# Scaling dO and making half of the first group's A products on GpSimd instead of VectorE

## The chip, the cores and the metric

The kernel runs on one core of one Trainium2 chip. The metric is the device time in microseconds of one launch. Its engines are TensorE (PE in the profile, with its weight loads listed apart as PEld), VectorE (DVE), ScalarE (ACT), GpSimd (POOL) and SyncE (SP), which here only issues DMAs.

## The reference

The forward function mixes two branches by a gate; the kernel computes the output and the gradients with respect to all weights and x, given `grad_out` (dO). S = 2048 tokens, D = 576, F = 4608, all inputs in bf16.

```python
def _A_ref(x, w_r, w_i):
    X = rfft2(x.astype(float32), axes=(-2, -1))
    X = X * (w_r + 1j * w_i)
    return irfft2(X, s=(S, D), axes=(-2, -1)).astype(bfloat16)

def _B_ref(x, w_gate, w_up, w_down):
    return (gelu(x @ w_gate) * (x @ w_up)) @ w_down

g = sigmoid((x * gate_w).sum(-1, keepdims=True))
out = g * _A_ref(x, w_r, w_i) + (1 - g) * _B_ref(x, w_gate, w_up, w_down)

out, vjp = jax.vjp(f, x, w_r, w_i, w_gate, w_up, w_down, gate_w)
return out, *vjp(grad_out)
```

In branch B, with `A = gelu(x w_gate) * (x w_up)`, the gradient of `w_down` is `A^T ((1 - g) dO)`. This is where the scaled dO and the A product, the two things that the change moves, meet.

## The kernel before

**The layout.** The 2048 tokens are 16 row tiles of 128 (T = 16). `xn` holds x and `dB` holds dO in this layout, each 128 x 16 x 576 in SBUF. Both are transposed at the start by TensorE into `xT` and `dOT`; the transposes of `dB` are done by 50 us.

**The head** (to about 55 us) builds the tables for the Fourier transforms (`build_D`, `build_R`, `build_B`: most of it on VectorE, a part of `build_D` on GpSimd), transposes x and dO, computes the first half of the forward transform of x, and the gate g with `omg32` = 1 - g in f32, one column per row tile.

**The first phase** loops over 18 groups g of 256 hidden columns (`NG`, `FG`), and within a group over four steps m (`NPR`), each of which handles four row tiles as two pairs, tp = 2m and 2m + 1. A step does this:
- `H_mm` puts the matmuls of z = dO w_down^T and of the two products x w_gate and x w_up (`xy`) on TensorE's queue.
- `H_da` scales z by `omg32` on ScalarE (line 345).
- `H_q` and `H_ew1` square and copy `xy` on ScalarE and start the polynomial of the gelu on VectorE (lines 351 to 361).
- `H_ew2` (lines 372 to 393) runs two sigmoids on ScalarE and then eight VectorE instructions for each pair: lines 380 to 387, in this order. Line 382 makes `xb` = gelu(x w_gate), line 383 makes `A` = `xb` * `hu`, and lines 384 to 387 make the two other results, `dHg` and `dHu`. A later `flush` stores all three to HBM from SyncE's queue.
- Units of the Fourier branch (`fft_next`) are put between these. In the first group they are those of `fwd_units`: two matmul sets `u1` (line 492) and `u2` (lines 506 to 509) per row tile. A `u1` result is copied out of PSUM by ScalarE (line 498). A `u2` result is copied out by VectorE for the first eight row tiles (line 512, `Vt`) and by ScalarE for the others. In the first group there are four such units per step and more in the first.

The order on each engine is the order in which this program writes the instructions; there is no scheduler. In the first group there is no other work. From the second group on, each step also runs units of the weight gradients of the group before (`W_units`): `u_dw` and `tail` (lines 442 and 455), and `u_dwd` (line 425), which multiplies A by the scaled `dB`. Their results leave through GpSimd's DMA queue (lines 435, 448, 461, 462), which is the only thing that GpSimd does in that stage. The first `u_dwd` runs in step m = 1 of the second group, at 121.55 us in the trace.

**The scaling of dO.** `u_dwd` needs `dB` multiplied by `omg32`, in place. `scale_dB(n)` (line 793) does this for the next n row tiles, one instruction of 128 x 576 each (line 795). The kernel calls it twice, for eight tiles each: at the end of step m = 3 of the first group and at the end of step m = 0 of the second:

```python
if (g, m) in ((0, 3), (1, 0)):
    scale_dB(T // 2)
```

**The second phase** starts after 1010 us: it reads A, dHg and dHu back from HBM, transposed, and computes the outputs with long chains of matmuls (line 950).

Of the kernel before, what the change touches and what calls it, by code (L numbers as in the profile page):

```python
# [10 lines left out]
ALU = mybir.AluOpType  # L11
# [9 lines left out]
P, T = 128, 16  # L21
# [151 lines left out]
def kernel(  # L173
# [4 lines left out]
    nc = tc.nc  # L178
    LD = nc.sync
    ST = nc.gpsimd  # L180
    V = nc.vector
# [26 lines left out]
    dB = wstack.enter_context(tc.tile_pool(name="pdB", bufs=1)).tile([P, T, D], BF16, name="dB")  # L208
# [58 lines left out]
    omg32 = res.tile([P, T], F32, name="omg32")  # L267
# [42 lines left out]
    def H_mm(g, m):  # L310

        wgu, wdT = wts[g]
        ts = range(4 * m, 4 * m + 4)
        z = pz.tile([P, 2, 2, FG], F32, tag="z", name="z")

        def zo(t):
            return z[:, t % 2, t % 4 // 2, :]
        for t in ts:
            for ci in range(4):
                nc.tensor.matmul(zo(t), lhsT=dOT[:, ci, t, :], rhs=wdT[:, ci, :], start=(t % 4 < 2 and ci == 0), stop=False)  # L320
        for t in ts:
            r = (LO, HI)[t % 2]
            nc.tensor.matmul(zo(t), lhsT=dOT[r, 4, t, :], rhs=wdT[r, 4, :], start=False, stop=t % 4 >= 2)  # L323
        xy = [ph.tile([P, 2, 2 * FG], F32, tag="xy", name="xy") for _ in range(2)]
        for t in ts:
            r = (LO, HI)[t % 2]
            nc.tensor.matmul(xy[t % 4 // 2][:, t % 2, :], lhsT=xT[r, 4, t, :], rhs=wgu[r, 4, :], start=True, stop=False)  # L327

        def full(k):
            for t in ts[2 * k:2 * k + 2]:  # L330
                for ci in range(4):
                    nc.tensor.matmul(xy[k][:, t % 2, :], lhsT=xT[:, ci, t, :], rhs=wgu[:, ci, :], start=False, stop=(ci == 3))  # L332
            return xy[k]
        return z, full

    def ewt(tag):
        return ew.tile([P, TPB, FG], BF16, tag=tag, name=tag, bufs=3 if tag in ("da", "xb") else 2)

    def H_da(m, z):
        das = []  # L340
        for k in range(2):
            da = ewt("da")
            for tt in range(TPB):
                t = 4 * m + 2 * k + tt
                nc.scalar.activation(da[:, tt, :], z[:, tt, k, :], ACT.Copy, scale=omg32[:, t:t + 1])  # L345
            das.append(da)
        return das

    def H_q(xy):
        q = ewt("q")  # L350
        nc.scalar.activation(q[:], xy[:, :, 0:FG], ACT.Square)  # L351
        return q

    def H_ew1(xy, q):
        xb, s, hu = (ewt(n) for n in ("xb", "s", "hu"))
        nc.scalar.copy(xb[:], xy[:, :, 0:FG])  # L356
        nc.scalar.copy(hu[:], xy[:, :, FG:2 * FG])
        V.tensor_scalar(s[:], q[:], A_GELU, 1.0, op0=ALU.mult, op1=ALU.add)  # L358
        V.tensor_tensor(s[:], xb[:], s[:], op=ALU.mult)  # L359
        V.tensor_scalar(q[:], q[:], 6.0 * A_GELU * C_GELU, 2.0 * C_GELU, op0=ALU.mult, op1=ALU.add)  # L360
        V.tensor_tensor(q[:], xb[:], q[:], op=ALU.mult)
        return xb, q, s, hu
# [3 lines left out]
    def flush(n=9):  # L366

        while stores and n:
            stores.pop(0)()
            n -= 1  # L370

    def H_ew2(g, tp, tiles, da):
        xb, q, s, hu = tiles
        om = ewt("om")
        nc.scalar.activation(om[:], s[:], ACT.Sigmoid, scale=-2.0 * C_GELU)  # L375
        nc.scalar.activation(s[:], s[:], ACT.Sigmoid, scale=2.0 * C_GELU)  # L376
        A = keepA.tile([P, TPB, FG], BF16, tag="A", name="A")
        dHg = keep.tile([P, TPB, FG], BF16, tag="dHg", name="dHg")
        dHu = keep.tile([P, TPB, FG], BF16, tag="dHu", name="dHu")
        V.tensor_tensor(om[:], om[:], q[:], op=ALU.mult)  # L380
        V.tensor_scalar(om[:], om[:], 1.0, None, op0=ALU.add)
        V.tensor_tensor(xb[:], xb[:], s[:], op=ALU.mult)
        V.tensor_tensor(A[:], xb[:], hu[:], op=ALU.mult)
        V.tensor_tensor(om[:], om[:], s[:], op=ALU.mult)
        V.tensor_tensor(om[:], om[:], hu[:], op=ALU.mult)
        V.tensor_tensor(dHg[:], da[:], om[:], op=ALU.mult)
        V.tensor_tensor(dHu[:], da[:], xb[:], op=ALU.mult)
        fsl = slice(g * FG, (g + 1) * FG)
        def store():
            for k, tl in enumerate((A, dHg, dHu)):  # L390
                LD.dma_start(scr[k][tp][:, :, fsl].rearrange("t p f -> p t f"), tl[:])
        stores.append(store)
        kept.setdefault(g, []).append((A, dHg, dHu))
# [366 lines left out]
    def fft_next():  # L760
        while fft_pos[0] < len(fft):
            u = fft[fft_pos[0]]
            fft_pos[0] += 1
            u()
            if not getattr(u, "noslot", False):
                return
# [6 lines left out]
    def want(pr):  # L773

        n0 = 4 * NPR
        n = 4 * (pr + 1) if pr < NPR else n0 + (n_slots - n0) * (pr + 1 - NPR) / (LASTP - NPR)
        return int(min(n, n_slots) + 1e-9)
# [14 lines left out]

    def scale_dB(n):
        for t in range(scaled[0], min(scaled[0] + n, T)):
            V.tensor_scalar(dB[:, t, :], dB[:, t, :], omg32[:, t:t + 1], None, op0=ALU.mult)
            scaled[0] = t + 1

    for g in range(NG):
        if g == 1:
            pgs.close()  # L800
            pw = ps1.enter_context(tc.tile_pool(name="pw", bufs=2, space=PSUM, **kw))
        for m in range(NPR):
            pr = g * NPR + m
            n = want(pr) - done[0]
            done[0] += n
            hs = [h for u in pend[m] for h in u] if pend else []

            def side_work():
                for _ in range(3):
                    if side:  # L810
                        side.pop(0)()
            if g == 0 and m > 0:
                fft_next()
            z, xy_full = H_mm(g, m)
            xy = xy_full(0)
            das = H_da(m, z)
            q = H_q(xy)
            flush()
            if n:
                fft_next()  # L820
                n -= 1
            if pr == 0:
                fft_next()
            ta = H_ew1(xy, q)
            state = []

            def sig0():
                H_ew2(g, 2 * m, ta, das[0])
                side_work()
                state.append(None)  # L830

            def second():
                xy = xy_full(1)
                if g == 0:
                    fft_next()
                state.insert(0, H_ew1(xy, H_q(xy)))

            def sig1():
                H_ew2(g, 2 * m + 1, state[0], das[1])
                side_work()  # L840
            if g == 0:
                second()
                fft_next()
                sig0()
                sig1()
            else:
                jobs = [(0, sig0)] * bool(carry) + carry + [(1.7, second)] + [(0, sig0)] * (not carry) + hs
                us = sum(j[0] for j in jobs)
                at, k, late = 0.0, 1, [sig1]
                for w, f in jobs:  # L850
                    if k <= n and at > 0 and at >= k * us / (n + 1) - 0.6:
                        fft_next()
                        k += 1
                        if len(state) == 2 and late:
                            late.pop()()
                    f()
                    at += w
                while k <= n:
                    fft_next()
                    k += 1  # L860
                if late:
                    sig1()
            carry = []
            flush(len(stores) - 1)
            if m < 3 and g + 1 < NG:
                load_w(g + 1, m)
            if pr == 3:
                LD.dma_start(gwb[:], gate_w.partition_broadcast(P))
            if (g, m) in ((0, 3), (1, 0)):
                scale_dB(T // 2)  # L870
            if done[0] == n_slots or (pr >= wgT_from and pr % 2 == 0 and len(wgT_all) < 20):
                load_wgT()
                if done[0] == n_slots:
                    load_wgT()
        carry = pend[4] if pend else []
        pend = W_units(g)
# [223 lines left out]
```

## Time and profile before

The median of three runs is 1461.26 us (1460.99 to 1462.75). The profiled execution spans 1460.1 us.

| engine | busy us | share of the span |
|---|---|---|
| PE (matmuls) | 1429.2 | 98% |
| PEld (weight loads) | 1065.0 | 73% |
| DVE | 846.9 | 58% |
| ACT | 686.8 | 47% |
| POOL | 119.1 | 8% |

By stretches of about one step of the first group, and one after it (busy us of each engine):

| stretch, us | PE | DVE | ACT | POOL |
|---|---|---|---|---|
| 64 to 75 | 10.21 | 10.00 | 9.30 | 0.00 |
| 75 to 85 | 9.60 | 9.48 | 8.30 | 0.00 |
| 85 to 95 | 9.10 | 9.45 | 8.29 | 0.00 |
| 95 to 105 | 8.77 | 9.64 | 7.18 | 0.00 |
| 105 to 115 | 9.84 | 9.49 | 6.16 | 1.84 |

The instructions that the change touches are the 16 of line 795, 360 to 366 ns each, the first eight at 101.8 us and the last at 115.5, and the 144 of line 383 (8 a group, 424 to 427 ns), the first at 66.0 us.

How to read the views: the chain of work that ended last is followed back from the last instruction of the program, at each step to what released it, or to the instruction before it on its engine; its list in order of time gives start, length, engine, the tile written and the line. A timeline gives start, length, engine, line, operation, the tiles written and read, shapes and the count of instructions merged into the row, and in brackets the idle time of the engine ahead of it and what ended that. Successive instructions of one engine may overlap a little in the records. Two things that the program did at once stand in two timelines, one for each engine.

### The profile page before, as it was taken

How to read it: one execution, taken by the hardware profiler on the slowest of the kernel's cores; microseconds unless marked ns; L12 is line 12 of the kernel's file. 1: busy time of each engine (PE TensorE's matmuls, PEld its weight loads, DVE VectorE, ACT ScalarE, POOL GpSimd, SP SyncE). 2: the span in 40 equal slices, each digit the busy share in tenths (PEclk: the TensorE clock that was granted, in tenths of full speed). 3: DMA queues.
4: the chain of work that ended last, by engine and by line, in shares of the span. 5: the costliest groups of instructions: out<-in, count | busy, mean ns of one | idle time of the engine just before them, and what ended most of it. 6: DMA issues, size and time to landing. Idle time of an engine off the chain costs nothing.

```text
span 1460.1 us, 29983 instructions
## 1 busy us (share of the span) xinstructions
PE 1429.2 (98%) x11691; PEld 1065.0 (73%) x11776; DVE 846.9 (58%) x2258; ACT 686.8 (47%) x1355; POOL 119.1 (8%) x203
## 2 busy tenths in 40 slices
PE   7999999999999999999999999999999999999998
PEld 5766777667777677677677677768877777777776
DVE  7697677888887986777777776773000531212100
ACT  5776666766676666766766766662000000000000
POOL 1000011011011101001001000100000100000000
PEclk9999999999999999999999999999999999999999
DMA  5244344555445445434543544657999997788773
GB/s 191 63 125 123 114 126 120 140 146 139 137 138 150 119 116 138 129 107 111 142 128 102 139 127 122 173 135 165 262 193 199 219 199 162 170 157 165 153 151 72
DMA packets 501161, 210.54 MB, mean 144 GB/s; under 512 B 320951, under 2 KB 491129, under 8 KB 501017
## 3 DMA queue, kind: packets, MB, share of 16 engines
q1 hardware_dynamic: 491416, 188.10, 54.3%
q0 software_dynamic: 7792, 19.49, 4.4%
q8 instruction: 92, 1.51, 0.5%
q10 hardware_dynamic: 1808, 1.02, 0.3%
q14 instruction: 53, 0.43, 0.1%
HBM read 40.89 MB, written 93.82 MB: 92 GB/s over the span
## 4 chain that ended last, share of the span: by engine, by line
PE 91%; DVE 4%; issue 1%; ACT 1%; DMA 0%; DVEq 0%; ACTq 0%
PE acc L950 29%; PE wps L442 17%; PE xy L332 16%; PE wps L425 9%; PE z L320 8%; PE wps L455 2%; PE xy L327 2%; PE z L323 1%; PE pf L707 1%; PE pf L681 1%; PE pf L492 1%; PE pf L709 1%; PE fx L492 0%; DVE Vt L512 0%; DMA pin<-scr 0%
## 5 line engine op out<-in xcount | busy, mean ns | idle before, releaser
L950 PEld LDWEIGHTS <-pin 128*128 128x128 bf16 x3456 | 337.9, 98 | 87.0 <-DMA pin<-scr 2.0
L332 PE MATMUL xy<-wgu,xT 128*128 128x512 bf16 x1067 | 258.5, 379 | 9.4 <-issue 7.3
L442 PEld LDWEIGHTS <-xn 128*128 128x128 bf16 x2304 | 225.3, 98 | 32.4 <-issue 0.2
L332 PEld LDWEIGHTS <-xT 128*128 128x128 bf16 x1152 | 106.8, 98 | 137.3 <-issue 30.3
L345 ACT ACTIVATE da<-z,omg 128x256 bf16<-128x256 f32 x288 | 113.4, 475 | 147.4 <-PE z L323 144.3
L967 ACT COPY bo<-acc 128x288 f32<-128x288 f32 x32 | 12.8, 400 | 309.8 <-PE acc L950 309.8
L425 PE MATMUL wps<-dB,A 128*128 128x288 bf16 x1152 | 154.2, 286 | 0.0
L950 PE MATMUL acc<-wd_all,pin 128*128 128x288 bf16 x1152 | 142.9, 286 | 1.4 <-DMA pin<-scr 0.9
L950 PE MATMUL acc<-wgT,pin 128*128 128x288 bf16 x1152 | 143.6, 286 | 0.0
L950 PE MATMUL acc<-wuT,pin 128*128 128x288 bf16 x1152 | 143.6, 286 | 0.0
L320 PE MATMUL z<-wdT,dOT 128*128 128x256 bf16 x1152 | 137.7, 273 | 2.2 <-ACT Y L498 1.2
L425 PEld LDWEIGHTS <-A 128*128 128x128 bf16 x1152 | 112.7, 98 | 35.7
L442 PE MATMUL wps<-dHg,xn 128*128 128x256 bf16 x1152 | 134.4, 273 | 0.0
L442 PE MATMUL wps<-dHu,xn 128*128 128x256 bf16 x1152 | 131.5, 273 | 0.0
L320 PEld LDWEIGHTS <-dOT 128*128 128x128 bf16 x1152 | 111.2, 98 | 19.7 <-issue 6.5
L1024 DVE SCALAR_TENSOR_TENSOR f32t<-gwf,dlog,b16t 128x576 f32<-128x576 f32 x16 | 13.1, 818 | 186.1 <-DMA b16t<-dxa_scr 186.1
L351 ACT ACTIVATE q<-xy 128x512 bf16<-128x512 f32 x144 | 86.1, 598 | 70.1 <-PE xy L332 65.7
L375 ACT ACTIVATE om<-s 128x512 bf16<-128x512 bf16 x144 | 92.0, 639 | 9.5 <-DVE s L359 9.3
L358 DVE TENSOR_SCALAR s<-q 128x512 bf16<-128x512 bf16 x144 | 42.9, 298 | 90.7 <-ACT q L351 88.5
L376 ACT ACTIVATE s<-s 128x512 bf16<-128x512 bf16 x144 | 90.7, 630 | 4.6
L448 POOL DMA_DIRECT2D out_dram<-dw x67 | 48.8, 729 | 537.3 <-ACT dw L403 259.8
L359 DVE TENSOR_TENSOR s<-xb,s 128x512 bf16<-128x512 bf16 x144 | 61.3, 426 | 44.4 <-ACT xb L356 38.1
(186 smaller groups left out, 1796.5 us busy)
## 6 DMA issues: line engine op xcount, KB each, us to landing
scr<-A SPq DMA_DIRECT2D x144, 128.0 KB, 2.1
scr<-dHg SPq DMA_DIRECT2D x144, 128.0 KB, 2.0
scr<-dHu SPq DMA_DIRECT2D x144, 128.0 KB, 2.0
out_dram<-dw POOLq DMA_DIRECT2D x67, 128.0 KB, 2.7
wd_all<-in_B_w_down_dram SPq DMA_DIRECT2D x3, 1728.0 KB, 15.2
out_dram<-dwd POOLq DMA_DIRECT2D x34, 144.0 KB, 2.2
wgu<-in_B_w_gate_dram SPq DMA_DIRECT2D x18, 256.0 KB, 3.0
wgu<-in_B_w_up_dram SPq DMA_DIRECT2D x18, 256.0 KB, 3.1
```

The lines of the kernel that those rows point to most:

```text
L320: nc.tensor.matmul(zo(t), lhsT=dOT[:, ci, t, :], rhs=wdT[:, ci, :], start=(t % 4 < 2 and ci == 0), stop=False)
L332: nc.tensor.matmul(xy[k][:, t % 2, :], lhsT=xT[:, ci, t, :], rhs=wgu[:, ci, :], start=False, stop=(ci == 3))
L345: nc.scalar.activation(da[:, tt, :], z[:, tt, k, :], ACT.Copy, scale=omg32[:, t:t + 1])
L351: nc.scalar.activation(q[:], xy[:, :, 0:FG], ACT.Square)
L358: V.tensor_scalar(s[:], q[:], A_GELU, 1.0, op0=ALU.mult, op1=ALU.add)
L359: V.tensor_tensor(s[:], xb[:], s[:], op=ALU.mult)
L375: nc.scalar.activation(om[:], s[:], ACT.Sigmoid, scale=-2.0 * C_GELU)
L376: nc.scalar.activation(s[:], s[:], ACT.Sigmoid, scale=2.0 * C_GELU)
L425: nc.tensor.matmul(wps[:, :288], lhsT=tl(0, t)[:, fch * P:(fch + 1) * P], rhs=dB[:, t, h * 288:(h + 1) * 288], start=(t == 0), stop=(t == ...
L442: nc.tensor.matmul(wps[:, cc, :], lhsT=xn[:, t, (c0 + cc) * P:(c0 + cc + 1) * P], rhs=tl(k, t), start=(t == 0), stop=(t == T - 1))
L448: wst[0].dma_start(ov[:, c0:c0 + TPB, fsl], dw[:])
L950: nc.tensor.matmul(acc[:, :288], lhsT=src[:, r, :], rhs=w_of(r)[:, h * 288:(h + 1) * 288], start=(first and r == 0), stop=(last and r == F ...
```

## The change

The change moves elementwise work of the first group from VectorE to GpSimd, an engine that has nothing to do there. All 16 scalings of `dB` go to GpSimd, four at the end of each of the first group's four steps instead of two batches of eight. In the first group, the A product of the even pair of each step goes there too (`tp % 2 == 0`), which is four of the group's eight. The other A products, those of the odd pairs and of all later groups, stay on VectorE. Nothing that is computed changes.

```diff
@@ H_ew2
         V.tensor_tensor(xb[:], xb[:], s[:], op=ALU.mult)
-        V.tensor_tensor(A[:], xb[:], hu[:], op=ALU.mult)
+        (nc.gpsimd if g == 0 and tp % 2 == 0 else V).tensor_tensor(A[:], xb[:], hu[:], op=ALU.mult)
         V.tensor_tensor(om[:], om[:], s[:], op=ALU.mult)
@@ scale_dB
         for t in range(scaled[0], min(scaled[0] + n, T)):
-            V.tensor_scalar(dB[:, t, :], dB[:, t, :], omg32[:, t:t + 1], None, op0=ALU.mult)
+            nc.gpsimd.tensor_scalar(dB[:, t, :], dB[:, t, :], omg32[:, t:t + 1], None, op0=ALU.mult)
             scaled[0] = t + 1
@@ for g ... for m ...
-            if (g, m) in ((0, 3), (1, 0)):
-                scale_dB(T // 2)
+            if g == 0:
+                scale_dB(4)
```

In the order of instructions, GpSimd's queue gets, between a memset of the head and the first DMA of the weight gradients, four times one A product and four scalings. VectorE's loses four instructions of line 383 and the two batches of line 795. TensorE's, ScalarE's and SyncE's stay the same.

## The prediction

> **What bounds the kernel now.** I read the busy shares and the chain's shares on the page first, then the chain in order of time around the first group, then the timelines of VectorE, TensorE and GpSimd there, and last the first ten microseconds, the only place where GpSimd and VectorE both compute.
>
> The page:
>
> ```profile
> PE 1429.2 (98%) x11691; PEld 1065.0 (73%) x11776; DVE 846.9 (58%) x2258; ACT 686.8 (47%) x1355; POOL 119.1 (8%) x203
> ...
> PE 91%; DVE 4%; issue 1%; ACT 1%; DMA 0%; DVEq 0%; ACTq 0%
> ```
>
> TensorE is the bound of the program, but 4% of the chain, some 58 us, is VectorE's. The chain in order of time tells where most of that lies:
>
> ```profile
> 64.90 0.43 DVE om L380
> ...
> 101.43 0.42 DVE dHu L387
> 101.85 2.24 DVE dB L795 x8
> 104.09 0.68 DVE Vt L512
> 104.81 1.40 PE pf L492 x10
> ```
>
> From 64.9 to 104.8 us the chain stays on VectorE: every piece left out here is a VectorE instruction or a few hundredths of "issue". That is exactly the elementwise work of the first group's four steps. In it VectorE never waits for another engine, so what is taken from it or put into it moves the line-512 copy at 104.09, on which TensorE sits idle for 0.95 us (PE timeline: the line-492 matmuls at 104.81 are released by Vt, line 512). From 104.8 on the chain is TensorE's.
>
> The VectorE timeline inside a step:
>
> ```profile
> 75.82 0.42 DVE L382 TENSOR_TENSOR xb<-xb,s 128x512 bf16<-128x512 bf16 x1
> 76.28 0.42 DVE L383 TENSOR_TENSOR A<-xb,hu 128x512 bf16<-128x512 bf16 x1
> 76.62 0.42 DVE L384 TENSOR_TENSOR om<-om,s 128x512 bf16<-128x512 bf16 x1
> ```
>
> Instructions overlap: starts are what count. A dependent product starts 0.46 us after its source (75.82 to 76.28), an independent one 0.34 us after the one ahead (76.28 to 76.62). A step takes 10.25 us (A of the even tile pair starts at 66.02, 76.28, 86.53, 96.78). TensorE is busy 9.10 us of the ten from 85 to 95, so it could keep a shorter step.
>
> The head of the program, GpSimd and then VectorE:
>
> ```profile
> 3.92 0.60 POOL L105 TENSOR_SCALAR yD<-lrow,dn 128x289 f32<-128x289 f32 x1
> 4.60 0.52 POOL L106 TENSOR_SCALAR yD<-yD 128x289 f32<-128x289 f32 x1
> ...
> 5.82 1.20 POOL L521 MEMSET At<- 128x1156 bf16 x1
> ```
>
> ```profile
> 3.62 1.21 DVE L108 SCALAR_TENSOR_TENSOR XD<-lrow,dcol,yD 128x289 f32<-128x289 f32 x2
> 4.86 0.87 DVE L111 SCALAR_TENSOR_TENSOR yD<-XD 128x578 f32<-128x578 f32 x1
> 5.65 1.52 DVE L105 TENSOR_SCALAR yD<-lrow,dn 128x289 f32<-128x289 f32 x2
> ...
> 7.71 0.95 DVE L108 SCALAR_TENSOR_TENSOR XD<-lrow,dcol,yD 128x289 f32<-128x289 f32 x2
> 8.69 0.76 DVE L111 SCALAR_TENSOR_TENSOR yD<-XD 128x578 f32<-128x578 f32 x1
> ```
>
> The same pair of line-108 instructions takes 1.21 us beside GpSimd's line 105 and 0.95 us alone; line 111 takes 0.87 us beside line 106 and 0.76 us alone. The second VectorE line-105 instruction, 0.35 us elsewhere, runs to 7.17, 0.15 us past the end of GpSimd's memset at 7.02. VectorE is held back while GpSimd works, and goes on the moment it ends.
>
> **What the Trainium skill says.** "SBUF — State Buffer", section "Who interferes with whom": VectorE and GpSimd share a pair of ports by an exclusive lock; a VectorE instruction with two SBUF inputs contends with a GpSimd one that reads SBUF, a single-source one in a two-port mode contends too, and the later one is blocked until the other is through. The head agrees (0.26 and 0.11 us added to two-input instructions), and shows that the two engines alternate there. "GPSIMD Engine Reference", section 3.1, prices a two-input elementwise product at about 2.6 cycles an element at 1.2 GHz; no row of this trace shows one. "Perfetto Trace Analysis", section "GPSIMD Engine Instruction", calls reported GpSimd spans unreliable; here their ends fit VectorE's to a few hundredths, so I use ends, not spans.
>
> **The change part by part.**
>
> Removed from VectorE, A products: four, one a step. Line 384 needs only om and s, so it then starts 0.34 us behind line 382 instead of 0.46 + 0.34 = 0.80 us: 0.46 us a step, 1.8 us in all, on the path.
>
> Removed, scalings: two batches of eight. The first (2.24 us on the chain) stands directly ahead of the line-512 copy that TensorE waits for: all of it on the path as long as VectorE is late there. The second, 113.56 to 115.79, I cost at nothing: TensorE is the bound there, and VectorE idles 3.25 us for ScalarE's q before 128.67.
>
> Added on GpSimd: in each step one A product, then four scalings, in that order on its queue; it had nothing there between 7 and 109 us. It has time for that: five instructions in 10 us. Their own lateness costs nothing: scaled dO and A are first read at 121.55 us (line 425), and the stores that come later on this queue begin at 109.39. New waits: A waits for line 382 (the four scalings are queued behind it, nobody waits for them soon); the store of A and those of dHg and dHu behind it wait for GpSimd, with nothing needing them; ScalarE may refill hu only after A is read, two tile pairs later. All cost nothing.
>
> Added on VectorE: the port. The 12 VectorE instructions from line 384 of the even pair to line 387 of the odd pair are 11 products of two SBUF inputs and one single-source instruction (line 381), and follow one another without a gap, and the next PSUM copy (line 512), which would not contend, comes 5 us after A. So GpSimd's five instructions fall among contending ones.
> - One scaling, 576 elements. Holding times in the head: line 105 can begin when the first line-108 instruction ends, 3.62 + 0.52 = 4.14, and ends at 4.52: 0.38 us for 289 elements; line 106 from 4.83 to 5.12: 0.29. That is 1.0 to 1.3 ns an element. Delays: 0.26 and 0.11. The holding is shortened by some 0.15 us, which VectorE spends between instructions anyway. For 287 elements more I add 0.29 to 0.37: 0.40 to 0.63 us, and take 0.52.
> - One A, 512 elements: an estimate from the page, 512 x 2.6 / 1.2 GHz = 1.11 us, less 0.15: 0.96. Bounds: 0.70 (the same page allows one operand a cycle, 1024 / 1.2 GHz = 0.85, less 0.15) and 1.3, which takes no gap off and adds a fifth.
>
> A step: 4 x 0.52 + 0.96 - 0.46 = +2.58 us; four steps +10.3; less the first batch of 2.24: the line-512 copy at 104.09 comes 8.1 us later, and TensorE, which waits for it already, with it. Everything behind is TensorE-bound, and gives nothing back. 1461.3 + 8.1 = 1469.4 us.
>
> With the bounds: 4 x 0.40 + 0.70 - 0.46 = 1.84 a step gives +5.1 (1466.4); 4 x 0.63 + 1.3 - 0.46 = 3.36 gives +11.2 (1472.5).
>
> **The rivals.**
> - No contention with bf16 products: VectorE only loses work. The line-512 copy would come 4 x 0.46 + 2.24 = 4.1 us sooner, but TensorE can use only its idle 0.95 us and the three shorter steps ahead of it, 3 x 0.46: 2.3 us, 1459.0. For it: the head shows f32 only, and bf16 products read half the bytes. Against it: they have two SBUF inputs all the same. Chance 0.12. This ends on the other side: not slower.
> - GpSimd gives way: it gets in mostly between instructions, and a scaling costs what line 106 did, some 0.15 to 0.2 us, A 0.3. Then 4 x 0.2 + 0.3 - 0.46 = 0.64 a step, x 4 - 2.24 = +0.3: 1461.6. For it: 0.11 us for line 106, and VectorE's instructions are closer together here. Against it: 0.26 for line 105, which like the scalings takes a scalar from a tensor. Chance 0.12.
> - Heavier GpSimd: four scalings without waits between them keep the port as one block, or bf16 is slower there: the reported spans 0.52 to 0.60 us for 289 elements, doubled, are 1.04 to 1.2. With a delay of 1.05 and A at 1.3: 4 x 1.05 + 1.3 - 0.46 = 5.04, x 4 - 2.24 = +17.9: 1479.2. Against it: the ends in the head fit shorter holds. Chance 0.14.
> - The forecast, contention in turn: 0.62.
>
> **How the numbers follow.** The forecast's bounds are 1466.4 to 1472.5. To leave out no more than 2 in 10 the range takes in most of the second rival's upper side and the lower half of the heavy one: 1462 to 1477. 0.2% is 2.9 us. Faster than 1458.3 needs the first rival at its best: 0.04. Within 0.2%: the rest of it, and most of the second: 0.16. Slower: 0.80.
>
> **What would show each step.** In the changed profile: five GpSimd instructions a step, and the even pairs' VectorE instructions from line 384 on stretched from 0.42 to about 1 us, A's neighbour most; the step at 12 to 13.5 us instead of 10.25; line 512's copy straight behind line 387 with no line 795 between; TensorE idle in the first group up by about 8 us, and from there on the same times as before, only later. VectorE durations still at 0.42 beside GpSimd would prove the forecast wrong, as would a step of 9.8 us; scalings of 1.1 us that hold VectorE throughout would speak for the heavy rival.

## The result, and the profile after

The changed kernel takes 1467.22 us (median of four runs, 1465.99 to 1470.23), the kernel before beside it 1461.74. The ratio is 1.004, with a 95% interval of 1.0023 to 1.0057: some 5.5 us slower, where 8.1 us were forecast. The page of the profile after, busy times and shares of the chain:

```profile
PE 1438.9 (98%) x11776; PEld 1065.0 (73%) x11776; DVE 850.0 (58%) x2238; ACT 686.5 (47%) x1355; POOL 152.7 (10%) x223
...
PE 91%; DVE 4%; ACT 1%; DMA 1%; issue 1%; SPq 0%; DVEq 0%; ACTq 0%
```

VectorE has 20 instructions fewer and 3.1 us more busy time. The instructions that stayed have become longer by more than the ones that left took. GpSimd gained 33.6 us. (TensorE's 9.7 us more come with 85 matmul records that the trace before lacks: 11691 of 11776.) The VectorE timeline of one step after (start, length, line, operation):

```profile
77.67 0.42 DVE L382 TENSOR_TENSOR xb<-xb,s 128x512 bf16<-128x512 bf16 x1
78.00 0.42 DVE L384 TENSOR_TENSOR om<-om,s 128x512 bf16<-128x512 bf16 x1
78.46 1.26 DVE L385 TENSOR_TENSOR om<-om,hu 128x512 bf16<-128x512 bf16 x1
79.75 0.85 DVE L386 TENSOR_TENSOR dHg<-da,om 128x512 bf16<-128x512 bf16 x1
80.52 0.41 DVE L387 TENSOR_TENSOR dHu<-da,xb 128x512 bf16<-128x512 bf16 x1
...
81.53 0.88 DVE L382 TENSOR_TENSOR xb<-xb,s 128x512 bf16<-128x512 bf16 x1
...
83.23 0.88 DVE L385 TENSOR_TENSOR om<-om,hu 128x512 bf16<-128x512 bf16 x1
...
86.22 0.44 DVE L360 TENSOR_SCALAR q<-q 128x512 bf16<-128x512 bf16 x1
```

and GpSimd's in the same step:

```profile
78.17 1.26 POOL L383 TENSOR_TENSOR A<-xb,hu 128x512 bf16<-128x512 bf16 x1 [3.75 <-DVE xb L382]
79.42 7.10 POOL L795 TENSOR_SCALAR dB<-dB,omg 128x576 bf16<-128x576 bf16 x4
```

Read the two side by side. Line 384 now follows line 382 directly (78.00), which is the saving. Line 385 takes 1.26 us instead of 0.42 and ends at 79.72, 0.29 us after GpSimd's A has ended at 79.43: it waited for A, 0.84 us. Then each of the four scalings makes one VectorE instruction longer: line 386 by 0.43, line 382 by 0.46, line 385 by 0.46, line 360 by 0.15. The sum is 2.34 us, less the 0.46 saved: 1.88 us a step. Line 385 of the even pair starts at 66.35, 78.46, 90.55 and 102.64: steps of 12.1 us instead of 10.25.

A scaling is 1.77 us long on GpSimd, but makes a VectorE instruction longer by a quarter of that. The chain in order of time at the end of the first group:

```profile
104.79 0.35 DVE dHu L387
...
105.16 0.35 ACT da L345
105.53 0.48 ACT da L345
...
106.05 0.28 PE pf L506
...
110.18 1.24 PE pf L492 x10
```

The line-492 matmuls that started at 104.81 now start at 110.18, 5.37 us later, and from there on the chain is TensorE's, as before. But what released TensorE is not the line-512 copy. It is ScalarE's da, which waited for line 387 of the even pair, the last reader of the da buffer that it writes. ScalarE's timeline there:

```profile
105.16 0.84 ACT L345 ACTIVATE da<-z,omg 128x256 bf16<-128x256 f32 x2 [1.60 <-DVE dHu L387]
```

### The profile page after: what moved, and what is told of

The parts are those of the page before. It is cut to its first block, busy times and chain, and to the rows that moved or that the text cites. A ratio compares the mean times of both kernels' runs of the same rounds, so it can differ in the third digit from the quotient of the medians.

```text
span 1465.7 us, 30077 instructions
## 1 busy us (share of the span) xinstructions
PE 1438.9 (98%) x11776; PEld 1065.0 (73%) x11776; DVE 850.0 (58%) x2238; ACT 686.5 (47%) x1355; POOL 152.7 (10%) x223
## 4 chain that ended last, share of the span: by engine, by line
PE 91%; DVE 4%; ACT 1%; DMA 1%; issue 1%; SPq 0%; DVEq 0%; ACTq 0%
PE acc L950 28%; PE wps L442 17%; PE xy L332 16%; PE wps L425 9%; PE z L320 8%; PE wps L455 2%; PE xy L327 2%; PE z L323 1%; PE pf L707 1%; PE pf L681 1%; PE pf L492 1%; DMA pin<-scr 1%; DVE om L385 1%; PE pf L709 1%; PE fx L492 0%
## 5 line engine op out<-in xcount | busy, mean ns | idle before, releaser
L332 PE MATMUL xy<-wgu,xT 128*128 128x512 bf16 x1152 | 271.4, 380 | 0.0
```

## The experiments

The theory after this result: VectorE waits for GpSimd's reading, not for the length of its instruction, and a reading costs what it lasts less some 0.15 us. The rivals: GpSimd's length counts, or each of its instructions has a fixed cost, or any activity of GpSimd does. A second question was what sets the pace of the first group, since the removed work brought less than its time. Each ratio is to the kernel before, measured beside it.

**A alone on GpSimd**, scalings as before.

```diff
-        V.tensor_tensor(A[:], xb[:], hu[:], op=ALU.mult)
+        (nc.gpsimd if g == 0 and tp % 2 == 0 else V).tensor_tensor(A[:], xb[:], hu[:], op=ALU.mult)
```

> The four A products on GpSimd alone, the scalings on VectorE as before. Theory (the read port is held for as long as GpSimd reads, about 1.1 us here): line 385 of each even pair is stretched by 0.84 us as in the changed kernel, 0.46 us is saved, so a step takes 10.63 us instead of 10.25 and the time is 1.5 us above the kernel before. Rival (only the scalings do harm, and a product fewer on VectorE is a gain): a step of 9.8 us and 1.4 us below.

Measured: ratio 1.0012 (1.0005 to 1.0018), 1.8 us slower. A starts at 77.67 and 88.30: a step of 10.63 us. Line 385 of the even pairs takes 1.26 us, the other products keep 0.42. The product is a loss by itself.

**Scalings alone on GpSimd**, A on VectorE.

```diff
-            V.tensor_scalar(dB[:, t, :], dB[:, t, :], omg32[:, t:t + 1], None, op0=ALU.mult)
+            nc.gpsimd.tensor_scalar(dB[:, t, :], dB[:, t, :], omg32[:, t:t + 1], None, op0=ALU.mult)
...
-            if (g, m) in ((0, 3), (1, 0)):
-                scale_dB(T // 2)
+            if g == 0:
+                scale_dB(4)
```

> The 16 scalings on GpSimd alone, four a step, all A products on VectorE. Theory: three VectorE products a step wait 0.45 us each for a scaling's reading and a fourth instruction 0.15 to 0.45: a step of 11.75 to 12.0 us; with the first batch of 2.24 us gone from VectorE the time is 3.7 to 4.8 us above before, and with the A run it adds up to the change's 5.5. Rival (VectorE is held for the scalings' whole length, 1.77 us each, and the A product only hid it): a step above 15 us and over 15 us above.

Measured: ratio 1.0031 (1.0019 to 1.0043), 4.5 us slower, as the theory has it; over 15 us is out. One thing in the expectation was wrong: without an A product between them nothing spaces the scalings out, so they ran one after another from 56.98 us to 85.33, in two steps instead of four. The sum of their waits can still be read. The line-512 copy before which the first batch stood starts at 107.27 instead of 104.00, 3.27 us later. Of this, 0.89 us were there before the first scaling: the last instruction of the gate (line 305) starts at 56.64 instead of 55.75, for a reason that is not in the edit. With the batch of 2.24 us gone from VectorE, 16 scalings cost 3.27 - 0.89 + 2.24 = 4.6 us, 0.29 each; this mean includes those that met an idle VectorE or a copy out of PSUM and cost nothing. The two parts add up to 6.3 us against 5.5 for the change, within their intervals.

**Scalings alone, in halves** of 288 columns (the calls of `scale_dB` as in the run before).

```diff
-            nc.gpsimd.tensor_scalar(dB[:, t, :], dB[:, t, :], omg32[:, t:t + 1], None, op0=ALU.mult)
+            for h in (slice(0, 288), slice(288, D)):
+                nc.gpsimd.tensor_scalar(dB[:, t, h], dB[:, t, h], omg32[:, t:t + 1], None, op0=ALU.mult)
```

> As the run with the scalings alone, but each in two halves of 288 columns, 32 instructions. Theory (the wait is the reading, 1.03 ns an element, less 0.15 us that VectorE spends between instructions anyway): 0.15 us a half where two products meet it, eight a step, 1.2 us: a step of 11.4 us, 2.6 us above before, less than with whole scalings. Rival (a fixed cost of some 0.45 us for each GpSimd instruction that VectorE meets): 3.4 us a step, over 11 us above before.

Measured: ratio 1.0023 (1.0016 to 1.0029), 3.4 us slower. Two VectorE products that met a half:

```profile
67.05 0.64 DVE L384 TENSOR_TENSOR om<-om,s 128x512 bf16<-128x512 bf16 x1
...
68.18 0.61 DVE L386 TENSOR_TENSOR dHg<-da,om 128x512 bf16<-128x512 bf16 x1
```

They are 0.19 to 0.22 us longer than 0.42, about half of what a whole scaling adds, and more than the 0.15 expected. The same line-512 copy starts at 105.98, 1.98 us later than before, of which 0.49 us were there ahead of the first scaling (line 305 at 56.24): 1.98 - 0.49 + 2.24 = 3.7 us for 32 halves, 0.12 each on the mean. A fixed cost per instruction is out: twice the instructions do not cost more in all. The time is 0.8 us above the 2.6 expected.

**Writing only**: memsets into a tile that has been read for the last time, added to the kernel before.

```diff
         V.tensor_tensor(dHu[:], da[:], xb[:], op=ALU.mult)
+        if g == 0 and tp % 2 == 0:
+            for _ in range(8):
+                nc.gpsimd.memset(om[:], 0.0)
```

> The kernel before, with eight GpSimd memsets of 128x512 bf16 added after line 386 of each even pair of the first group, into the om tile that nobody reads any more: they write and read nothing. Theory (two-input products wait for the read port only): the products keep 0.42 us; only the single-source instructions (line 381, perhaps 358 and 360) may wait, up to 0.5 us each, one or two a step: 0 to 3 us above before. Rival (any GpSimd instruction holds VectorE while it runs): eight times 0.4 us a step, 13 us above.

Measured: ratio 1.002 (1.0013 to 1.0027), 2.9 us slower; a step takes 10.80 us. GpSimd, then VectorE in that step:

```profile
78.95 4.63 POOL L390 MEMSET om<- 128x512 bf16 x8 [6.17 <-DVE dHg L386]
```

```profile
79.15 0.42 DVE L380 TENSOR_TENSOR om<-om,q 128x512 bf16<-128x512 bf16 x1
79.60 0.61 DVE L381 TENSOR_SCALAR om<-om 128x512 bf16<-128x512 bf16 x1
...
80.57 0.43 DVE L383 TENSOR_TENSOR A<-xb,hu 128x512 bf16<-128x512 bf16 x1
...
83.17 0.56 DVE L358 TENSOR_SCALAR s<-q 128x512 bf16<-128x512 bf16 x1
```

While GpSimd writes without a break from 78.95 to 83.58, every two-input product keeps its 0.42 us, the copy out of PSUM (line 515 here) keeps its 0.75, and the two instructions with a single SBUF source take about 0.3 us more each. So writing alone does not hold the products, and it does hold single-source instructions; whether reading alone would hold those too was not tried. This fits the page "SBUF — State Buffer", section "Who interferes with whom", as cited in the prediction, seen with its two sides apart. What the section says of the length, that the later instruction is blocked until the other is through, is not what the change shows: beside a scaling of 1.77 us a product took only 0.43 to 0.46 us more.

**GpSimd alone**, added in the second phase where VectorE is nearly idle.

```diff
             V.tensor_copy(dlog_bf[:, t:t + 1], dlog[:, t:t + 1])
+            n = (D, D, 288, 288)[t % 4]
+            src = (do_t, diff)[t % 2]
+            ds = (b16t, f32t)[t % 2]()
+            nc.gpsimd.tensor_scalar(ds[:, :n], src[:, :n], dlog[:, t:t + 1], None, op0=ALU.mult)
+            ds2 = b16t()
+            nc.gpsimd.tensor_tensor(ds2[:, :512], do_t[:, :512], a_t[:, :512], op=ALU.mult)
```

> The kernel before, with GpSimd work added in the second phase where VectorE is nearly idle: after each output tile's last VectorE instruction a scaling (by turns 576 bf16, 576 f32, 288 bf16, 288 f32 columns) and a product of 512 bf16 columns, into tiles that nobody reads. Theory (the long scalings are GpSimd's own pace): 576 bf16 columns take 1.7 us here too, the product 1.2 us. Rival (they are long because they wait for VectorE): 576 columns take about 0.7 us, the product 1.1.

GpSimd's timeline of this run:

```profile
1131.31 1.73 POOL L995 TENSOR_SCALAR b16t<-b16t,dlog 128x576 bf16<-128x576 bf16 x1 [1.04 <-DVE dlog L990]
1133.03 1.15 POOL L997 TENSOR_TENSOR b16t<-b16t 128x512 bf16<-128x512 bf16 x1
...
1151.78 1.00 POOL L995 TENSOR_SCALAR b16t<-b16t,dlog 128x288 bf16<-128x288 bf16 x1 [1.07 <-issue]
```

While VectorE is idle the scaling is as long, 1.73 us, so it is not long because of VectorE; f32 gives 1.72 too. In tiles where VectorE worked beside it, 576 columns took up to 2.04 us. But in the head 289 columns took 0.52 to 0.60, not 1.00. Those had two operations.

**GpSimd alone, other forms** (from a tensor, with plus 0, by a constant).

```diff
+            k = t % 4
+            nc.gpsimd.tensor_scalar(ds[:], do_t[:], 2.0 if k == 2 else dlog[:, t:t + 1], 0.0 if k in (1, 3) else None,
+                                    op0=ALU.mult, **({"op1": ALU.add} if k in (1, 3) else {}))
...
```

> As the run with GpSimd alone in the second phase, with other forms: by turns a scaling of 576 bf16 columns by a number from a tensor, the same with a second operation (plus 0), by a constant, and again with the second operation; then 512 columns by a number from a tensor. Theory (the form with one operation is slow in GpSimd's program): 1.7 us with one operation, some 0.7 to 1.1 us with two, as in the head, where 289 columns with two operations took 0.52 to 0.60. Rival (the length goes with columns alone, 2.5 ns each): 1.7 us for all of 576.

```profile
1271.79 1.72 POOL L994 TENSOR_SCALAR b16t<-b16t,dlog 128x576 bf16<-128x576 bf16 x1 [1.00 <-DVE dlog L990]
...
1298.41 0.74 POOL L994 TENSOR_SCALAR b16t<-b16t,dlog 128x576 bf16<-128x576 bf16 x1 [1.01 <-DVE dlog L990]
...
1323.71 1.66 POOL L994 TENSOR_SCALAR b16t<-b16t 128x576 bf16<-128x576 bf16 x1
```

The rows are those of three successive output tiles: by a number from a tensor 1.72 us, the same plus zero 0.74 (1.04 to 1.06 in three tiles where VectorE's line 979 ran beside it), by a constant 1.66. The second operation makes it shorter. The constant form did not run alone: it does not need the result of line 990, so it started earlier, and VectorE's line 987, an f32 instruction with two inputs, took 1.46 us beside it instead of 0.76. That is a wait of 0.70 us, so the 0.43 to 0.46 of the first group is no fixed price of a scaling.

**The change with the two-operation form**: the sharpest test of reading against length.

```diff
-            nc.gpsimd.tensor_scalar(dB[:, t, :], dB[:, t, :], omg32[:, t:t + 1], None, op0=ALU.mult)
+            nc.gpsimd.tensor_scalar(dB[:, t, :], dB[:, t, :], omg32[:, t:t + 1], 0.0, op0=ALU.mult, op1=ALU.add)
```

> The changed kernel with the scalings in the two-operation form (times omg, plus 0), which took 0.74 us alone on GpSimd instead of 1.72. Theory (VectorE waits for GpSimd's reading, 0.59 us in either form): four two-input products a step wait 0.43 to 0.46 us each instead of three and a lesser fourth, a step of 12.1 to 12.4 us, 5.4 to 6.5 us above before: the shorter form brings nothing. Rival (the length of GpSimd's instructions is what costs): less than half of the scalings' part, a step of 11.2 us or less and under 3 us above before.

Measured: ratio 1.0036 (1.0023 to 1.005), 5.2 us slower, and a step of 12.24 us (A at 79.02 and 91.26). GpSimd's scalings of one step, then VectorE beside them:

```profile
80.27 3.93 POOL L795 TENSOR_SCALAR dB<-dB,omg 128x576 bf16<-128x576 bf16 x4
```

```profile
80.60 0.85 DVE L386 TENSOR_TENSOR dHg<-da,om 128x512 bf16<-128x512 bf16 x1
...
81.71 0.88 DVE L380 TENSOR_TENSOR om<-om,q 128x512 bf16<-128x512 bf16 x1
82.62 0.72 DVE L381 TENSOR_SCALAR om<-om 128x512 bf16<-128x512 bf16 x1
...
83.70 0.77 DVE L383 TENSOR_TENSOR A<-xb,hu 128x512 bf16<-128x512 bf16 x1
```

The four scalings are done in 3.93 us instead of 7.10, and VectorE still loses 0.35 to 0.46 us to each, 1.67 us in a step against 1.50 with the long form. One of the four is line 381, not a product as expected. The step is as expected; the time is 0.2 us below the range. Length as the cause is out. That it is GpSimd's reading that holds the products is an inference from three runs: the wait goes with the columns (halves) and not with the length (this run), and writing alone does not cause it (memsets). No view shows when an instruction reads.

**One late batch**: all 16 scalings on VectorE, in the second group.

```diff
-            if (g, m) in ((0, 3), (1, 0)):
-                scale_dB(T // 2)
+            if (g, m) == (1, 0):
+                scale_dB(T)
```

> All 16 scalings on VectorE in one batch at the end of step m = 0 of the second group. Theory: the copy that TensorE waits for comes 2.24 us sooner, TensorE gains its 0.95 us of idle time, and the longer batch is hidden behind TensorE's work: 0.9 us below before. Rival (VectorE is not free in the second group): the elementwise work of its step m = 0 or 1 comes late, 1 to 2 us above.

Measured: ratio 0.9995 (0.9989 to 1.0002), by time not to be told from before. In the trace the line-512 copy starts at 101.75 instead of 104.00, but the line-492 matmuls start at 103.85 instead of 104.81: TensorE has its 0.95 us, and no more, of the 2.24 us that VectorE was freed of.

**The late batch, and every second Vt copy on ScalarE.**

```diff
-                if src is xT or t < 8:
+                if src is xT or (t < 8 and t % 2 == 0):
```

> As the run with one late batch of scalings, and of the copies Vt of dO's transform in the first group every second one goes to ScalarE. Theory (VectorE sets the pace of the first group): a step loses 0.67 us, to 9.6 us, so TensorE gains three times that and the 0.95 us: 2.5 to 3 us below before. Rival (ScalarE, busy 8.3 of 10 us, takes over as the bound with 0.6 us more in a step): about the 0.9 us of the late batch alone, or nothing.

Measured: ratio 0.9989 (0.9983 to 0.9996), 1.1 us faster than before; the 2.5 to 3 us of the theory did not come. The intervals of this run and of the late batch overlap, and in the trace the first group ends alike (line 492 at 103.84): VectorE has 0.67 us less to do in a step, and the step is still 10.25 us (line 380 at 75.15 and 85.40). Its chain in order of time:

```profile
84.10 0.74 ACT Y L498
84.85 0.53 ACT om L375
...
85.40 0.44 DVE om L380
...
88.20 0.35 DVE dHu L387
...
88.57 0.85 ACT da L345 x2
...
89.46 1.40 PE pf L492 x10
```

This is a loop through ScalarE, VectorE and TensorE, closed by 4.9 us of TensorE's work up to the next Y at 94.35. Line 512 is not in it.

**The late batch, and a fourth buffer for da**, which takes away what the loop waits for; then **both**.

```diff
-        return ew.tile([P, TPB, FG], BF16, tag=tag, name=tag, bufs=3 if tag in ("da", "xb") else 2)
+        return ew.tile([P, TPB, FG], BF16, tag=tag, name=tag, bufs={"da": 4, "xb": 3}.get(tag, 2))
```

> As the run with one late batch of scalings on VectorE, and a fourth buffer for da, so that ScalarE's scaling of z need not wait for line 387. Theory (two things tie at 10.25 us a step: VectorE's own work, and the loop line 498 - sigmoid - lines 380 to 387 - da - TensorE): with the loop cut alone VectorE still needs 10.25 us, and the time is that of the late batch, 0.7 to 1.1 us below before. Rival (the loop alone is the bound): a step of 9.7 us and 2.5 to 3 us below before.

> The same with every second Vt copy on ScalarE too, so that both things that tie are cut. Theory: a step of 9.6 to 9.7 us, 2.5 to 3.3 us below before (ratio 0.998). Rival (something else, TensorE's or ScalarE's own order, also needs 10.25 us): as the late batch alone, 0.7 to 1.1 us below.

Measured: the late batch with the fourth buffer 0.9992 (0.9983 to 1.0), a step of 10.23 us (line 380 at 75.11 and 85.34): cutting the loop alone leaves VectorE's own 10.2 us. With both, 0.9987 (0.998 to 0.9993), about 1.9 us faster than before, and a step of 10.05 us instead of the 9.6 to 9.7 expected:

```profile
74.44 1.91 PE L320 MATMUL z<-wdT,dOT 128*128 128x256 bf16 x16 [0.34 <-ACT Y L498]
84.50 1.91 PE L320 MATMUL z<-wdT,dOT 128*128 128x256 bf16 x16 [0.34 <-ACT Y L498]
```

Now TensorE itself fills the step, but for its wait for ScalarE's copy of Y out of the PSUM buffer that z takes next. So three things lie within 0.2 us of each other: VectorE's own work, the loop through da, and TensorE's work with its wait for Y. The last kernel is faster than both kernels of this case.

## Why the prediction was right, and where a term was off

- **VectorE is held by GpSimd, and the added waits reach the end**: right. The chain runs on VectorE through the group, with 2.34 us of waits in each step, and the 5.37 us at line 492 are those of the result. What the prediction read in the head, that VectorE goes on the moment GpSimd's instruction ends, does not hold for a scaling: line 386 has ended at 80.60, while the first of the four scalings, by their mean length, runs to about 81.2. Nor do the lines of the head show ends that fit "to a few hundredths": VectorE's instructions end 0.31 us (4.83 against 4.52) and 0.15 us (7.17 against 7.02) after GpSimd's.
- **One scaling costs 0.52 us**: too much; this is the largest term that was mis-sized. Three of four cost 0.43 to 0.46, at the low end of the 0.40 to 0.63 given, and the fourth 0.15, a mean of 0.37. An estimate of the reading: if the first scaling reads from the end of line 385, 79.72, and line 386, which ends at 80.60, was let go 0.29 us before its end, as line 385 was by A, then it was let go at 80.31. That is a reading of 0.59 us, about 1.0 ns a column, and a gap of 0.15 as assumed. The fourth was cheap because of what it met: a scaling lasts 1.77 us, so by their mean length it began at about 84.75, together with line 512's copy out of PSUM (84.82), which kept its 0.75 us; the 0.15 of line 360 came at its end. "GpSimd's five instructions fall among contending ones" therefore held for four.
- **A costs 0.96 us**: 0.84; the price of 2.6 cycles an element in "GPSIMD Engine Reference", section 3.1, 1.11 us, agrees with the 1.15 us that the product takes while VectorE is idle.
- **A step +2.58 us**: 1.85 to 1.88, by these two terms.
- **All of the first batch, 2.24 us, is on the path**: wrong, and hidden by an error the other way. The late batch shows that only 0.95 us of it is TensorE's to gain. But the fourth step's waits didn't all count either: TensorE was released by da behind line 387 of the even pair, so what came after that line was off the path. At the end of the third step the line-512 copy is 5.40 us late (96.91 against 91.51), the fourth adds some 0.92 up to line 387, TensorE's former idle time of 0.95 goes: 5.37. The prediction's sum with the measured step, 4 x 1.85 - 2.24, gives 5.2, nearly the same for another reason: that the two errors cancel is luck.
- **What is taken from VectorE moves the end**: wrong beyond the 0.95 us. Its uninterrupted chain was one of three things that take about 10.1 to 10.25 us; the run with the Vt copies shows that less VectorE work alone shortens no step. The rival without contention, at 2.3 us gained, was too hopeful as well. The trace before had the sign of it, in ScalarE's timeline of each step:

```profile
98.83 0.84 ACT L345 ACTIVATE da<-z,omg 128x256 bf16<-128x256 f32 x2 [0.56 <-DVE dHu L387]
```

ScalarE stands idle there for line 387, and TensorE takes up its next matmuls (99.72) right behind.
- **GpSimd's lateness and the second batch cost nothing**: nothing in the traces speaks against it. The z matmuls of the second group's second step start 5.21 us later than before (115.03 against 109.82), no more than line 492 does.

## What to carry to other kernels

GpSimd is not a free helper for VectorE's two-input products: price an offload by what it adds to the VectorE instructions that run beside it, and compare that with what the instruction costs on VectorE. Here a scaling moved 0.28 us of VectorE work at a price of 0.37, and an A product 0.46 at 0.84. A chain that stays on one engine says that work added to it counts, as far as the chain stays there; it doesn't say that removed work does, since another loop may take as long.

## What the runs showed of the hardware that was not expected

- GpSimd's scaling of 576 bf16 columns takes 1.72 us with one operation and 0.74 us with two (the second adds zero), while VectorE is idle; 288 columns with one take 1.00. In the first group VectorE loses 0.35 to 0.46 us to a scaling of the short form, and 0.43 to 0.46 to one of the long form that meets a product.
- So the length in the profile is no measure of what a GpSimd instruction blocks: a scaling of 1.77 us made a product 0.43 to 0.46 us longer, an A product of 1.26 us made one 0.84 us longer.
- GpSimd's memsets left VectorE's two-input products untouched and lengthened its instructions with a single SBUF source by about 0.3 us each.
